# A new order for everything after the twentieth step of a fused attention and gated feed-forward kernel

## The chip, the cores and the metric

The kernel runs on one core of a Trainium2 chip. The metric is the device time of one execution in microseconds (us), as the median of several runs of the program. The core has five engines that each take their instructions in order from a queue of their own: PE (TensorE, matrix products; PEld is its loading of weights), DVE (VectorE), ACT (ScalarE), POOL (GpSimd) and SP (SyncE, which here only issues transfers). An engine whose next instruction waits for a semaphore does nothing else meanwhile, and all that stands behind that instruction waits too.

## The reference: what is computed

Two parts, one feeding the other. First a windowed attention with summaries of blocks of keys and values:

```python
k_sum = k.reshape(B, H, nb, block, D).max(axis=3)        # B, H, S, D = 4, 8, 768, 64; block 32
v_sum = v.reshape(B, H, nb, block, D).mean(axis=3)
scores_l = scale * np.matmul(q, k.transpose(0, 1, 3, 2)) # kept where |row - column| < 16
scores_s = scale * np.einsum('bhsd,bhnd->bhsn', q, k_sum) + np.log(block)
a = softmax(np.concatenate([masked scores_l, scores_s], axis=-1))
attn = np.matmul(a, np.concatenate([v, v_sum], axis=2))
```

Its output, 3072 tokens of 512 numbers, then goes through a feed-forward part with a gate that needs a cosine:

```python
h = x @ w_in            # (3072, 512) @ (512, 2048)
g = h * np.cos(h)
out = g @ w_out         # (3072, 2048) @ (2048, 512)
```

All of it is float32. (The code above is cut to what is computed.)

## The kernel before, in words

**Tiles.** The 3072 tokens are eight blocks of 384. For each block the attention is done by four groups (`Group`), one per pair of heads, named a, b, c, d with the block's number: c4 is the third pair of heads of block 4. The feed-forward part is done by 128 steps (`Step`), s0 to s127: a step is one block and one of the 16 slices of 128 columns of `w_in`. Blocks 0 and 1 share s0 to s31, then blocks 2 to 7 have 16 steps each: s48 to s63 are block 3, s80 to s95 block 5, s112 to s127 block 7. Products are taken with operands split into a high and a low part (`fp32r`), three products for one.

**What a step does.** `up` (L738) makes 12 products of 128x384 on PE into one bank of PSUM; this is `h`. Then follows a chain over two engines: `tu` (L748, ACT), `re` (L751, DVE), `si` (L756, ACT, the sine), `ga` (L760, DVE, the product with `h`), `hi` (the high part `gh`: L383 on ACT, or L385 on DVE) and `lo` (the low part `gl`: L389 on POOL or DVE). `dh` (L789) makes six products of 128x512 from `gh`, and `dl` three from `gl`, into three accumulating banks. At a block's last step `ta` (L825 on ACT, L827 on DVE) copies the three accumulators with a minus sign to SBUF, and `st` (L841) writes them out. The very last chunk is written in two halves (L845), one from SP's queue and one from ACT's. The tiles `t`, `gh` and `gl` have two buffers each, so that `hi` of a step can wait for `dh` of an earlier one.

**What a group does** (from block 2 on): `q` and `k` load, `qt` and `kt` (DVE) transpose, `kw` copies windows of the keys, `sc` (L581, PE) makes the scores, `z` (L601, DVE) scales and masks, `mx` (L614, DVE), `su` (L617, POOL), `ex` (L631, ACT), `sm` (L635, DVE), `iv` (L638, DVE) and `nm` (L641, POOL) are the softmax, `pt` (L664, DVE) transposes in squares of 32, `po` (L672) writes the result to DRAM, and `pi` (L679, four transfers) reads it back in another arrangement. `v` (L489 twice and L497 once) and `m` (L510, two transfers) load the values and their summaries into the tile `vn`. `va` (L694, PE) makes the attention's output, from which `xh` (L383 or L385) and `xl` (L389, DVE) are the two parts of `x` that the next block's `up` reads. The tiles `vn` and `pt` of these blocks have one buffer each: `v`, `m` and `pi` of one group cannot be issued before `va` of the group ahead has ended.

**What sets the order.** Nothing is scheduled automatically. A long string, `ORDER`, holds 2079 tokens such as `s22.dh.1.6.7` (step 22, first products of the down projection, in banks 1, 6 and 7) or `s23.lo.v` (low part of step 23 on VectorE), and a loop calls the method of each token in turn. Each engine gets its instructions in this order; the last part of a token names the banks of PSUM or the engine (`a` ACT, `v` DVE, `p` POOL).

```python
        for token in ORDER.split():
            who, what, *args = token.split(".")
            one = whose[who]
```

Of the kernel before, what the change touches and what calls it, by code (L numbers as in the profile page):

```python
# [67 lines left out]
s21.dh s21.dl s23.tu s23.re s21.ta.1.1.v s22.up.0 c2.ks.0 c2.kw.v c2.sc.7.2 a2.va.3 s21.st.1 d2.q b2.v s22.tu s23.si  # L68
s22.re s22.si s21.ta.2.0.v b2.sm s22.ga s21.st.2 s22.hi.a c2.z.0.v s23.ga b2.iv c2.z.1.v d2.ks.0 s22.lo.p b2.nm
d2.kw.a b2.pt.1 s26.up.4 s24.up.0 s24.tu c2.mx s24.re s23.hi.a s23.lo.v s27.up.2 s25.up.5 s26.tu s21.ta.0.0.v s24.si  # L70
s24.ga c2.su c2.ex s22.dh.1.6.7 s24.hi.v s22.dl s23.dh s23.dl s24.dh b2.m v2_2.l b2.po c2.sm s26.re s26.si s24.lo.p
v2_2.s.p b2.pi d2.qt a3.q v2_3.l s25.tu s25.re s25.si s24.dl c2.iv s26.ga s25.ga s25.hi.a d2.sc.0.4 b2.va.5 c2.v c2.m
a2.xh.a b2.xh.a d2.z.0.v d2.z.1.v c2.nm s25.lo.p s26.hi.v s27.tu c2.pt.1 s27.re s27.si s27.ga a3.kw.v b2.xl d2.mx
c2.po a3.qt v2_3.s.p v2_4.l c2.pi s21.st.0 s28.up.0 s31.up.4 s30.up.2 s29.up.5 d2.su d2.ex d2.sm d2.iv s26.lo.p
v2_4.s.v s28.tu s28.re d2.nm d2.pt.1 s25.dh s25.dl s27.hi.a s26.dh s26.dl s27.dh s27.lo.p s27.dl s28.si s28.ga s29.tu
s29.re s29.si s28.hi.v s29.ga s29.hi.v a2.xl s28.lo.p s31.tu a3.sc.0.5 c2.va.3 d2.po s31.fe.1.0 b3.q v2_5.l d2.m d2.pi
# [24 lines left out]
s54.tu s51.dh s51.dl s52.dh s52.dl d4.qt s53.ga s54.re s54.si d4.kw.a s53.hi.v s53.lo.v s53.dh c4.z.1.v s54.ga
s54.hi.a s54.lo.p s53.dl s54.dh c4.mx c4.su c4.ex c4.sm c4.iv d4.sc.0.1 d4.z.1.v a5.q b4.po v3_2.l a4.va.2 b4.m b4.v
s55.up.4 s55.tu c4.nm c4.pt.0 s55.re v3_2.s.v s55.si s55.ga s55.hi.a s59.up.1 s56.up.5 b4.pi v3_3.l s55.lo.p s57.up.4
a5.qt d4.z.0.v s56.tu s56.re s56.si s56.ga s56.hi.v s54.dl s56.lo.p a4.xh.a s55.dh s55.dl s56.dh s56.dl s59.tu s59.re
a5.kw.a a4.xl s57.tu s59.si s57.re s57.si b4.va.0 b4.xh.a d4.mx s57.ga s59.ga s59.hi.v a5.sc.2.4 b4.xl a5.z.1.v b5.q
b5.qt v3_3.s.p c4.v c4.m v3_4.l c4.po s58.up.1 c5.q d4.su d4.ex s59.lo.p d4.sm b5.kw.v d4.iv a5.z.0.v d4.nm s57.hi.a
s57.lo.v s58.tu s58.re a5.mx d4.pt.1 d4.po s58.si s62.up.0 s60.up.2 s60.tu s63.up.4 s61.up.5 s57.dh s58.ga s58.hi.v
s57.dl s58.dh s58.lo.v s58.dl s59.dh s59.dl s60.re s60.si s60.ga s60.hi.a s60.lo.v s62.tu s62.re s61.tu s61.re s61.si
s61.ga s61.hi.v s61.lo.v s62.si s62.ga s60.dh s62.hi.v s63.tu s63.re s63.si v3_4.s.p v3_5.l v3_5.s.p c4.pi c4.va.2
d4.v d4.m d4.pi b5.sc.5.1 b5.z.0.v c5.qt c4.xh.v v3_6.l s60.dl s62.lo.p s61.dh s61.dl s62.dh s62.dl s63.ga c4.xl a5.su  # L110
c5.kw.a a5.ex s63.hi.v s63.dh a5.sm s63.lo.p s63.dl c5.sc.0.2 a5.iv a5.nm a5.pt.0 a5.po d4.va.4 d4.xh.v d4.xl c5.z.0.v
# [5 lines left out]
s67.dl s68.dh s68.lo.p s70.tu s68.dl s70.re d5.sc.6.1 d5.z.1.v s70.si s70.ga c5.sm s70.hi.v a5.va.2 s70.lo.v a5.xh.a
a5.xl s69.up.1 s69.tu s69.re s69.si s73.up.0 s72.up.2 b5.m b5.v c5.iv d5.z.0.v s69.ga s69.hi.a s69.lo.p a6.ks.0
a6.ks.1 a6.kw.a s73.tu s69.dh s69.dl s70.dh s70.dl a6.qt s71.tu s71.re s71.si c5.nm c5.pt.1 d5.mx s71.ga s71.hi.a
s71.lo.v s72.tu s72.re s72.si s72.ga s72.hi.v b5.pi b5.va.6 b5.xh.v s72.lo.v d5.su d5.ex s73.re s73.si b6.kt.0 d5.sm  # L120
b6.kt.1 s73.ga a6.sc.3.1 a6.z.0.v s71.dh s71.dl s72.dh s72.dl s78.up.2 s76.up.0 s77.up.3 s76.tu s73.hi.a b5.xl
a6.z.1.v s76.re a6.mx b6.ks.1 s73.lo.p s76.si s76.ga s74.up.6 s74.tu d5.iv d5.nm s74.re s74.si s74.ga s74.hi.v
s74.lo.p s75.up.0 s75.tu s75.re s79.up.1 c5.po c5.m b6.q c5.v c6.k c5.pi c5.va.6 s73.dh s73.dl s74.dh s75.si s75.ga
s75.hi.a d5.pt.1 d5.po d5.m d5.v d5.pi s75.lo.p b6.ks.0 s77.tu s77.re s76.hi.a s74.dl s76.lo.v s77.si s78.tu c6.kt.0
s78.re s78.si s75.dh s75.dl s76.dh b6.qt s77.ga s77.hi.v s78.ga c6.kt.1 s78.hi.v s76.dl s77.lo.v s79.tu s79.re
# [869 lines left out]
```

## Time and profile before

| | |
|---|---|
| time before | 638.99 us, median of 3 runs: 634.86, 638.99, 639.19 |
| the profiled execution | span of 633.6 us from its first to its last instruction; 12128 instructions |
| PE | busy 620.6 us (98%) |
| DVE, ACT, POOL | busy 426.8 us (67%), 315.7 us (50%), 208.7 us (33%) |
| chain that ended last | 91% of the span on PE |
| PE's clock as granted | at least nine tenths of full speed in each of 40 slices; 1.00 on average over the stretches below |

The page gives the span of the profiled execution; its time with what lies around the span is not listed apart. The lowest of the three timed runs is 1.3 us above that span, the median 5.4 us. Matrix products overlap in the profile: one of 128x384 is listed with 337 ns, but the next starts about 175 ns later. So the time that PE needs for a piece of work is read from the chain of waits, where 12 of them take about 2.1 us, and not from the mean of one.

### The profile page before, as it was taken

The page shows a single profiled execution, that of the slowest core. Times are in us where ns is not written, and L with a number is a line of the kernel's source. Part 1 is how long each engine was busy: PE and PEld are TensorE (multiplying, and loading weights), DVE is VectorE, ACT ScalarE, POOL GpSimd, SP SyncE. Part 2 cuts the span into 40 slices and gives each one's busy share as a digit, 9 for nine tenths or more (in the row PEclk, how much of TensorE's full clock was granted, in tenths as well). Part 3 has the DMA queues.
Part 4 walks back from the last instruction along what each step waited for, and adds up shares of the span by engine and source line. Part 5 has one row for each costly group of instructions (what it writes and reads, how often), then busy time and mean ns, then how long its engine had stood idle before and what let it go on. Part 6 is the DMA issues. An engine that isn't in the chain of part 4 may idle for free.

```text
span 633.6 us, 12128 instructions
## 1 busy us (share of the span) xinstructions
PE 620.6 (98%) x4596; PEld 546.6 (86%) x4596; DVE 426.8 (67%) x795; ACT 315.7 (50%) x557; POOL 208.7 (33%) x243
## 2 busy tenths in 40 slices
PE   7889999999999999999999999999999999999997
PEld 5469898988889989897998989898888998989895
DVE  5689889986767877766766576657775555554524
ACT  3588776765544454464534554353554352522323
POOL 3136543563532523243434432211432241201000
PEclk9999999999999999999999999999999999999999
DMA  8987876734354465434343544232242313300001
GB/s 218 289 235 203 283 238 187 164 80 109 104 157 123 100 152 117 110 87 115 77 128 98 134 109 109 72 78 62 72 116 87 100 47 98 93 25 34 17 1 50
DMA packets 171305, 74.10 MB, mean 117 GB/s; under 512 B 136944, under 2 KB 160112, under 8 KB 171248
## 3 DMA queue, kind: packets, MB, share of 16 engines
q1 hardware_dynamic: 171104, 73.21, 43.6%
q8 instruction: 36, 0.59, 0.4%
q14 instruction: 21, 0.17, 0.1%
q10 hardware_dynamic: 144, 0.13, 0.1%
HBM read 54.43 MB, written 16.52 MB: 112 GB/s over the span
## 4 chain that ended last, share of the span: by engine, by line
PE 91%; SPq 3%; DVE 2%; DMA 2%; ACT 1%; POOL 0%; issue 0%; DVEq 0%; ACTq 0%
PE banks L738 41%; PE banks L789 41%; PE banks L694 4%; PE banks L581 3%; DMA late<-in_moe_w_out_dram 2%; SPq L468 2%; PE banks L650 1%; PE banks L593 0%; ACT L756 0%; SPq L497 0%; SPq L906 0%; SPq L489 0%; ACT t L756 0%; DVE t L760 0%; DVE xl L389 0%
## 5 line engine op out<-in xcount | busy, mean ns | idle before, releaser
L738 PE MATMUL banks<-xh,w 128*128 128x384 f32 x1024 | 267.0, 337 | 0.0
L789 PE MATMUL banks<-w,gh 128*128 128x512 f32 x768 | 197.4, 392 | 0.6 <-DVE stage L827 0.6
L738 PEld LDWEIGHTS banks<-xh,w 128*128 128x128 f32 x1024 | 185.3, 188 | 2.4 <-issue 1.3
L738 PE MATMUL banks<-xl,w 128*128 128x384 f32 x512 | 171.1, 334 | 0.0
L789 PEld LDWEIGHTS banks<-w,gh 128*128 128x128 f32 x768 | 142.7, 188 | 31.4 <-issue 1.2
L389 POOL TENSOR_TENSOR gl<-t,gh 128x384 fp32r<-128x384 f32 x67 | 68.7, 1029 | 240.2 <-DVE gh L385 84.6
L748 ACT ACTIVATE t<-banks 128x384 int32<-128x384 f32 x128 | 62.3, 489 | 162.4 <-PE banks L738 88.0
L751 DVE SCALAR_TENSOR_TENSOR t<-t,banks 128x384 f32<-128x384 int32 x128 | 69.7, 547 | 66.7 <-ACT t L748 66.3
L789 PE MATMUL banks<-w,gl 128*128 128x512 f32 x384 | 108.7, 391 | 0.0
L760 DVE TENSOR_TENSOR t<-t,banks 128x384 f32<-128x384 f32 x128 | 69.6, 548 | 41.9 <-ACT t L756 40.2
L756 ACT ACTIVATE t<-t 128x384 f32<-128x384 f32 x128 | 66.3, 523 | 63.0 <-DVE t L751 62.7
L738 PEld LDWEIGHTS banks<-xl,w 128*128 128x128 f32 x512 | 96.1, 188 | 0.3
L789 PEld LDWEIGHTS banks<-w,gl 128*128 128x128 f32 x384 | 71.8, 188 | 15.3 <-issue 0.2
L641 POOL TENSOR_TENSOR sc<-sc,r 128x720 f32<-128x720 f32 x28 | 40.1, 1432 | 58.6 <-DVE r L638 54.5
L383 ACT CAST gh<-t 128x384 fp32r<-128x384 f32 x62 | 31.4, 510 | 35.3 <-DVE t L760 19.2
L617 POOL TENSOR_TENSOR sc<-sc,m 128x720 f32<-128x720 f32 x24 | 34.0, 1415 | 44.5 <-DVE m L614 41.3
L389 DVE TENSOR_TENSOR gl<-t,gh 128x384 fp32r<-128x384 f32 x61 | 38.9, 640 | 11.5 <-ACT gh L383 6.6
L385 DVE CAST gh<-t 128x384 fp32r<-128x384 f32 x66 | 25.3, 383 | 15.8 <-PE banks L789 12.5
L254 POOL TENSOR_TENSOR kn<-kn 96x256 f32<-96x256 f32 (+1 forms) x38 | 25.7, 677 | 23.7 <-DMA kn<-in_v_dram 22.0
L601 DVE SCALAR_TENSOR_TENSOR sc<-banks,mask 128x360 f32<-128x360 f32 x48 | 24.2, 519 | 13.4 <-PE banks L581 13.4
L635 DVE TENSOR_REDUCE r<-sc 128x6 f32<-128x726 f32 x28 | 25.1, 897 | 10.0 <-ACT sc L631 9.6
L664 DVE STREAM_TRANSPOSE stage<-sc 128x768 f32<-128x768 f32 x24 | 23.3, 970 | 10.5 <-POOL sc L641 10.2
(115 smaller groups left out, 558.0 us busy)
## 6 DMA issues: line engine op xcount, KB each, us to landing
pd<-stage SPq DMA_DIRECT2D x24, 384.0 KB
late<-in_moe_w_out_dram SPq DMA_DIRECT2D x16, 511.6 KB
late<-in_moe_w_in_dram SPq DMA_DIRECT2D x16, 510.5 KB
pt<-pd SPq DMA_DIRECT2D x72, 96.0 KB
vn<-in_v_dram SPq DMA_DIRECT2D x50, 120.0 KB
out_dram<-stage SPq DMA_DIRECT2D x23, 256.0 KB
kn<-in_v_dram SPq DMA_DIRECT2D x24, 192.0 KB
qn<-in_q_dram SPq DMA_DIRECT2D x96, 48.0 KB
```

Source lines behind the costliest of these rows:

```text
L254: eng.tensor_tensor(out=t[:, :n], in0=t[:, :n], in1=t[:, n:], op=ALU.add)
L383: eng.copy(out=out, in_=in_)
L389: eng.tensor_tensor(out=lo, in0=src, in1=hi.bitcast(F32), op=ALU.subtract)
L617: nc.gpsimd.tensor_tensor(out=self.sc, in0=self.sc, in1=self.m.unsqueeze(2).broadcast_to([P, U, NK]), op=ALU.subtract)
L641: nc.gpsimd.tensor_tensor(out=self.sc, in0=self.sc, in1=self.r.unsqueeze(2).broadcast_to([P, U, NK]), op=ALU.mult)
L694: nc.tensor.matmul(out=self.xps[rows, t * QT : (t + 1) * QT], lhsT=self.vn[:, t, rows], rhs=self.pt[2 * c + hh][s], start=True, stop=True,)
L738: nc.tensor.matmul(out=self.h, lhsT=w_of(name, self.f)[:, c * P : (c + 1) * P], rhs=x_of(self.blk, part, c), start=n == 0, stop=n == last,)
L748: nc.scalar.activation(out=self.t.bitcast(I32), in_=self.h, func=AF.Copy, scale=1.0 / TWO_PI, bias=0.25)
L751: nc.vector.scalar_tensor_tensor(out=self.t, in0=self.t.bitcast(I32), scalar=-TWO_PI, in1=self.h, op0=ALU.mult, op1=ALU.add)
L756: nc.scalar.activation(out=self.t, in_=self.t, func=AF.Sin, scale=-1.0, bias=-0.5 * math.pi)
L760: nc.vector.tensor_tensor(out=self.t, in0=self.t, in1=self.h, op=ALU.mult)
L789: nc.tensor.matmul(out=self.acc[i], lhsT=g[:, i * P : (i + 1) * P], rhs=w_of(name, self.f), start=self.first and n == 0, stop=self.last an ...
```

## The change

From the token after `a2.va.3` on, all tokens stand in a new order up to the end; the 560 tokens ahead of that, which load and split the weights and do the steps up to s20 and most of s21, are as they were. The tokens are the same 2079 operations. With the new order some banks are others, and some of the operations that can run on two engines change sides: of the low parts (`lo`) 14 go from DVE to POOL and 13 from POOL to DVE, of the high parts (`hi`) 12 from ACT to DVE and 10 back, and five of the copies of key windows (`kw`) and four of the high parts of `x` (`xh`) change too. No function is changed, and no operation is added or removed. The first lines of the table that differ:

```diff
-s21.dh s21.dl s23.tu s23.re s21.ta.1.1.v s22.up.0 c2.ks.0 c2.kw.v c2.sc.7.2 a2.va.3 s21.st.1 d2.q b2.v s22.tu s23.si
+s21.dh s21.dl s23.tu s23.re s21.ta.1.1.v s22.up.0 c2.ks.0 c2.kw.v c2.sc.7.2 a2.va.3 s23.si s23.ga s23.hi.a s23.lo.v
```

Three places in the built programs are spoken of below. The first is DVE between the copies of key windows for c2 (`kw`) and the copy of the first accumulator of step 21 (L827, `stage_2002` before and `stage_1999` after). `gl` is the low part of step 23. Before, it is the last instruction ahead of that copy:

```order
L601 SCALAR_TENSOR_TENSOR sc<-banks,mask 128x3x120
L551 TENSOR_REDUCE kd_119<-kd_119 128x12
L664 STREAM_TRANSPOSE stage_1941<-sc 128x6x4x32
L614 TENSOR_REDUCE m<-sc 128x6
L751 SCALAR_TENSOR_TENSOR t<-t,banks 128x384
L389 TENSOR_TENSOR gl<-t,gh 128x384
L827 TENSOR_SCALAR stage_2002<-banks 128x512
```

In the changed program it follows the copies of the windows at once, behind the gate (L760) of the same step:

```order
L385 COPY kw<-kd_118 128x6x96
L385 COPY kw<-kd_118 128x6x24
L760 TENSOR_TENSOR t<-t,banks 128x384
L389 TENSOR_TENSOR gl<-t,gh 128x384
L751 SCALAR_TENSOR_TENSOR t<-t,banks 128x384
L635 TENSOR_REDUCE r<-sc 128x6
L760 TENSOR_TENSOR t<-t,banks 128x384
L827 TENSOR_SCALAR stage_1928<-banks 128x512
```

The same instructions stand between the window copies and the copy of that accumulator in both programs; the low part moved from their end to their start.

The second place is PE between the attention products of c4 and of d4 (L694, `va`), in block 4. L581 are scores of other groups; the products with `w_1347`, `w_1566`, `w_1718` and `w_1595` belong to steps 60, 61, 62 and 63. Before:

```order
L694 MATMUL banks<-pt,vn 64x64 x12
L581 MATMUL banks<-kw,qd 64x120 x12
L789 MATMUL banks<-w_1347,gl 128x512 x3
L789 MATMUL banks<-w_1566,gh 128x512 x6
L789 MATMUL banks<-w_1566,gl 128x512 x3
L789 MATMUL banks<-w_1718,gh 128x512 x6
L789 MATMUL banks<-w_1718,gl 128x512 x3
L789 MATMUL banks<-w_1595,gh 128x512 x6
L789 MATMUL banks<-w_1595,gl 128x512 x3
L581 MATMUL banks<-kw,qd 64x120 x12
L694 MATMUL banks<-pt,vn 64x64 x12
```

Now:

```order
L789 MATMUL banks<-w_1347,gl 128x512 x3
L581 MATMUL banks<-kw,qd 64x120 x12
L694 MATMUL banks<-pt,vn 64x64 x12
L789 MATMUL banks<-w_1566,gh 128x512 x6
L789 MATMUL banks<-w_1566,gl 128x512 x3
L789 MATMUL banks<-w_1718,gh 128x512 x6
L789 MATMUL banks<-w_1718,gl 128x512 x3
L789 MATMUL banks<-w_1595,gh 128x512 x6
L789 MATMUL banks<-w_1595,gl 128x512 x3
L581 MATMUL banks<-kw,qd 64x120 x12
L694 MATMUL banks<-pt,vn 64x64 x12
```

The scores of b5 and the low products of step 60 went ahead of c4's attention products, so that less of PE's work lies between those of c4 and those of d4. A row of 12 such products in this list is 24 in the trace.

The third place is the end of SP's queue, where the output is written. `stage_6593` and `stage_6596` before are chunks 0 and 1 of the last block, `last` the first half of chunk 2:

```order
L841 DMA out_dram<-stage_6221 128x512
L841 DMA out_dram<-stage_6083 128x512
L841 DMA out_dram<-stage_6346 128x512
L841 DMA out_dram<-stage_6593 128x512
L841 DMA out_dram<-stage_6596 128x512
L845 DMA out_dram<-last 128x256
```

Now `stage_6593` is chunk 1 and `stage_6600` chunk 0:

```order
L841 DMA out_dram<-stage_6133 128x512
L841 DMA out_dram<-stage_6083 128x512
L841 DMA out_dram<-stage_6513 128x512
L841 DMA out_dram<-stage_6593 128x512
L845 DMA out_dram<-last 128x256
L841 DMA out_dram<-stage_6600 128x512
```

The write of chunk 0 went from the third last place to the last, behind the half of the last chunk. The other half, on ACT's queue, is where it was.

More of the change, by code (lines that the diff above doesn't have):

```diff
@@ L72 @@
[L72 to L76, printed above, removed]
@@ L102 @@
[L102 to L106, printed above, removed]
@@ L107 @@
[L107 to L111, printed above, removed]
@@ L117 @@
[L117 to L121, printed above, removed]
@@ L122 @@
[L122 to L125, printed above, removed]
-s78.lo.v s77.dh s79.si s79.ga s79.hi.v b6.kw.a c5.xh.a s77.dl s78.dh s78.dl s79.dh a6.su s79.lo.p s79.dl c5.xl a6.ex
@@ L167 @@
-s126.re s124.hi.a s124.lo.v s125.tu s124.dh s124.dl s126.si s125.re s125.si s125.ga s125.hi.v s125.dh s126.ga
-s125.lo.v s126.hi.a s126.lo.v s127.tu s127.re s127.si s127.ga s125.dl s126.dh s126.dl s127.hi.v s127.dh s127.lo.v
-s127.dl s127.ta.0.0.v s127.st.0 s127.ta.1.1.a s127.st.1 s127.ta.2.a s127.st.2 s127.sb.2
+s21.dh s21.dl s23.tu s23.re s21.ta.1.1.v s22.up.0 c2.ks.0 c2.kw.v c2.sc.7.2 a2.va.3 s23.si s23.ga s23.hi.a s23.lo.v
+d2.q s22.tu s22.re s21.st.1 b2.sm s22.si s22.ga s21.ta.2.0.v s21.st.2 s22.hi.a s22.lo.p d2.ks.0 c2.z.0.v b2.iv b2.nm
@@ new lines @@
+c2.z.1.v d2.kw.a b2.pt.1 s26.up.4 s24.up.0 s24.tu s25.up.5 c2.mx s24.re s27.up.2 s26.tu s21.ta.0.0.v s24.si s24.ga
+c2.su c2.ex s22.dh.1.7.6 b2.v s24.hi.v s22.dl s23.dh s23.dl s24.dh v2_2.l b2.m b2.po s26.re s26.si s24.lo.p s24.dl
+d2.qt b2.pi v2_2.s.p v2_3.l s25.tu c2.sm a3.q c2.iv s26.ga s25.re s25.si d2.sc.0.4 s25.ga s25.hi.a b2.va.5 c2.v c2.nm
+c2.m b2.xh.a a2.xh.a s25.lo.p d2.z.0.v c2.pt.1 d2.z.1.v s26.hi.v s27.tu s27.re s27.si s27.ga a3.kw.v b2.xl d2.mx
+s28.up.0 v2_3.s.p a3.qt v2_4.l v2_4.s.v s21.st.0 s31.up.4 s30.up.2 d2.su c2.po d2.ex s29.up.5 d2.sm d2.iv c2.pi
@@ new lines @@
+s108.si s108.ga s108.hi.a s108.dh s108.lo.p s108.dl s110.tu s109.hi.v s109.dh s109.lo.p s109.dl s111.tu d7.v s110.re
+s110.si s110.ga s110.hi.a s110.lo.p c7.xh.v s110.dh c7.xl s111.re s111.si s111.ga s111.hi.v s110.dl s111.dh d7.m
+s111.lo.p s111.dl s111.ta.2.1.v d7.po d7.pi d7.va.3 d7.xh.v d7.xl s113.up.5 s113.tu s113.re s112.up.3 s111.ta.0.0.v
+s116.up.1 s114.up.4 s118.up.0 s112.tu s112.re s112.si s112.ga s112.hi.v s112.lo.p s116.tu s113.si s113.ga s113.hi.v
+s113.lo.p s116.re s116.si s116.ga s112.dh.6.2.3 s112.dl s113.dh s113.dl s116.hi.v s116.lo.v s114.tu s118.tu s115.up.5
@@ new lines @@
+s114.re s114.si s114.ga s114.hi.v s114.lo.v s118.re s115.tu s118.si s114.dh s114.dl s115.re s115.si s115.ga s115.hi.v
+s115.lo.p s117.up.1 s117.tu s117.re s115.dh s115.dl s116.dh s116.dl s117.si s117.ga s117.hi.v s117.lo.v s118.ga
+s118.hi.v s118.lo.p s120.up.5 s122.up.4 s123.up.0 s123.tu s119.up.1 s123.re s123.si s120.tu s117.dh s117.dl s111.st.0
+s120.re s123.ga s123.hi.v s123.lo.v s118.dh s118.dl s121.up.0 s119.tu s119.re s119.si s119.ga s119.hi.v s119.dh
+s119.lo.v s119.dl s120.si s120.ga s122.tu s126.up.1 s122.re s122.si s120.hi.a s120.lo.p s120.dh s121.tu s121.re
```

158 lines of the change are left out of this document (85 added, 73 removed).

## The prediction

> **What bounds the kernel now.** I read the page first, then a table of busy time by stretches, then PE's own waits.
>
> ```profile
> span 633.6 us, 12128 instructions
> PE 620.6 (98%) x4596; PEld 546.6 (86%) x4596; DVE 426.8 (67%) x795; ACT 315.7 (50%) x557; POOL 208.7 (33%) x243
> PE 91%; SPq 3%; DVE 2%; DMA 2%; ACT 1%; POOL 0%; issue 0%; DVEq 0%; ACTq 0%
> ```
>
> PE is busy almost throughout and is 91% of the chain that ended last. Where it is not busy matters most, so I cut the span into four stretches: the loading of weights, the rest of the unchanged part, the part that gets the new order, and what follows the last product. After the stretch's length come the busy times of PE, PEld, DVE, ACT and POOL, the granted clock, the share of the transfer engines and GB/s.
>
> ```profile
> 0.00:48.00 48.00, 40.07 (x645) 28.46 (x646) 34.37 (x73) 29.12 (x73) 13.33 (x42) 1.00 0.92 249
> 48.00:144.70 96.70, 96.70 (x616) 87.01 (x615) 86.08 (x139) 68.85 (x115) 52.16 (x50) 1.00 0.67 189
> 144.70:629.30 484.60, 483.80 (x3338) 431.17 (x3336) 306.30 (x585) 217.21 (x371) 143.22 (x151) 1.00 0.35 89
> 629.30:633.60 4.30, 0.00 (x0) 0.00 (x0) 0.00 (x0) 0.53 (x1) 0.00 (x0) 0.96 0.51 183
> ```
>
> In the third stretch, the only one with a new order, PE is busy 483.80 of 484.60 us at full clock. No product is added, removed or resized, so an order can win there only the 0.80 us of idle time, and perhaps a tenth or two in hidden short waits. It can lose as much as it likes. The 7.93 us of idle time before 48 us are out of its reach, and the 4.3 us behind the last product are touched only by the order of three writes. Of the 0.80 us, one wait makes 0.6 (us in total, times, longest):
>
> ```profile
> PE banks L789 <- DVE stage L827: 0.6, 1, 0.6
> ```
>
> **The change part by part.** First that wait. PE, DVE and POOL around it:
>
> ```profile
> 161.11 0.34 PE L738 MATMUL banks<-xh,w 128*128 128x384 f32 x1
> 162.06 1.62 PE L789 MATMUL banks<-w,gh 128*128 128x512 f32 x6 [0.62 <-DVE stage L827]
> 151.84 0.55 DVE L751 SCALAR_TENSOR_TENSOR t<-t,banks 128x384 f32<-128x384 int32 x1 [1.20 <-ACT t L748]
> 159.81 1.50 DVE L389 TENSOR_TENSOR gl<-t,gh 128x384 fp32r<-128x384 f32 x1
> 161.24 0.68 DVE L827 TENSOR_SCALAR stage<-banks 128x512 f32<-128x512 f32 x1
> 159.51 1.39 POOL L617 TENSOR_TENSOR sc<-sc,m 128x720 f32<-128x720 f32 x1 [1.88 <-DVE m L614]
> L389 DVE TENSOR_TENSOR gl<-t,gh 128x384 fp32r<-128x384 f32 x61 | 38.9, 640 | 11.5 <-ACT gh L383 6.6
> L383 ACT CAST gh<-t 128x384 fp32r<-128x384 f32 x62 | 31.4, 510 | 35.3 <-DVE t L760 19.2
> ```
>
> PE's products end at 161.45 and `dh` of s22 waits until the copy of the first accumulator of s21 has ended (161.92). Just ahead of that copy on DVE the low part of s23 took 1.50 us, where 61 of its kind have a mean of 640 ns; POOL ran a subtraction of 1.39 us from 159.51 on. In the new order the low part stands behind the copies of the key windows, 0.64 us long if POOL lets it, and the rest of the set before the accumulator's copy is the same. That alone frees 1.50 - 0.64 = 0.86 us, more than the 0.62 of the wait. Against that, DVE now stands still for the cast on ACT (510 ns) between gate and low part, but before it stood still at the same place for 1.20 us waiting for ACT. I take -0.6 us; the other end is +0.5, if that cast comes on top and the saving fails. Behind the moved low part are queued a residue and a sum on DVE; PE needs neither before the accumulator's copy.
>
> [...]
>
> Second, the loads of the values. `vn` and `pt` have one buffer, so for d4 nine transfers start after the products of c4. SP and PE before:
>
> ```profile
> 335.38 0.85 SPq L489 DMA_DIRECT2D vn<-in_v_dram  x2
> 336.29 0.48 SPq L497 DMA_DIRECT2D vn<-in_v_dram  x1
> 336.82 1.66 SPq L510 DMA_DIRECT2D vn<-vs  x2
> 338.60 1.84 SPq L679 DMA_DIRECT2D pt<-pd  x4
> 334.44 0.92 PE L694 MATMUL banks<-pt,vn 120*64 120x64 f32 x24
> 336.87 1.53 PE L789 MATMUL banks<-w,gh 128*128 128x512 f32 x6
> 343.86 0.92 PE L694 MATMUL banks<-pt,vn 120*64 120x64 f32 x24
> SPq L679 <- DMA pd<-stage: 12.1, 9, 2.1
> ```
>
> The products of c4 end at 335.36, the last issue at 338.60 + 1.84 = 340.44: 5.08 us of issuing. The landing has no row of its own. It is at most 343.86 - 340.44 = 3.42 us, since PE did not wait for it, and the nearest row is SP's wait for `pd`, at most 2.1 us. So 7.2 us are needed (5.1 to 8.5). In the new order the scores of b5 and three products of s60 no longer lie between, and what is left is the stretch from 336.87 to 343.86, 7.0 us. That is a wait of 0.2 us where 1.3 us were spare. The same happens once more, from b6 to c6: between them now stand scores, two steps of `dh` and `dl` and one `up`.
>
> ```profile
> 343.16 0.78 PE banks L581 x24
> 461.22 6.84 PE banks L789 x30
> 473.25 1.84 SPq L679 DMA_DIRECT2D pt<-pd  x4
> 469.68 8.52 PE banks L738 x48
> 468.98 1.73 SPq L510 DMA_DIRECT2D vn<-vs  x2
> ```
>
> 0.78 + 18 x 0.228 + 12 x 0.178 = 7.0 us. Before, the nine issues for c6 ran from 468.98 to 475.09, 6.1 us, while PE had until 469.68 + 8.52 = 478.2: at most 3.1 us for landing. With 5.1 + 2.1 = 7.2 the wait is 0.2, with 6.1 + 3.1 it would be 2.2. All other pairs of this kind have more of PE's work between them. From a6 to b6 there are 10.6 us (four `up` of 8.52 / 4 = 2.13, one step of 9 x 0.228 = 2.05), but two loads of b6's summaries now stand ahead of its `po` in SP's queue, and wait for a6. Two of them (1.66), `po` (0.4, as one write below), its landing (2.1), four and three more (1.84 + 1.33) and a landing (2.1) make 9.4: 1.2 to spare. I take +0.4 for all; the ends are 0 and 1.5 + 2.2 = 3.7.
>
> Third, the end. The write of chunk 0 is now behind the first half of chunk 2.
>
> ```profile
> 628.33 0.69 DVE L827 TENSOR_SCALAR stage<-banks 128x512 f32<-128x512 f32 x1 [1.44 <-PE banks L789]
> 629.05 0.81 SPq L841 DMA_DIRECT2D out_dram<-stage  x2
> 629.95 0.40 SPq L845 DMA_DIRECT2D out_dram<-last  x1
> 630.00:631.00 1.00, 0.00 (x0) 0.00 (x0) 0.00 (x0) 0.00 (x0) 0.00 (x0) 1.00 1.02 373
> 631.00:632.00 1.00, 0.00 (x0) 0.00 (x0) 0.00 (x0) 0.00 (x0) 0.00 (x0) 1.00 1.03 368
> ```
>
> Chunk 0 was ready at 629.02 and its issue began at 629.05; now it begins at 630.35. From issue to flowing data it is about 0.95 us (629.05 to 630.0), so its 256 KB flow from 631.3, and at some 370 GB/s they take 0.7 us: until 632.0, when the data ended before. But the engines idle a little at 630, as only chunk 1 is there. I take +0.2; ends 0 and 0.7, one whole chunk late.
>
> Fourth, shorter leads. From the end of `up` to `dh` of the same step the new order has eight steps with only two other steps' work (4.1 us) on PE between them: s56, s69, s80, s86, s95, s100, s110, s115. Before there are two, s69 and s118. How s69 went (ACT, DVE, PE):
>
> ```profile
> 373.78 0.49 ACT L748 ACTIVATE t<-banks 128x384 int32<-128x384 f32 x1 [1.81 <-DVE xl L389]
> 375.44 0.56 DVE L760 TENSOR_TENSOR t<-t,banks 128x384 f32<-128x384 f32 x1
> 376.03 0.52 ACT L383 CAST gh<-t 128x384 fp32r<-128x384 f32 x1 [0.62 <-DVE t L760]
> 377.69 1.08 PE L789 MATMUL banks<-w,gh 128*128 128x512 f32 x4
> L756 ACT ACT_TABLE_LOAD x23 | 29.5, 1283 | 0.4
> L631 ACT ACTIVATE sc<-sc 128x720 f32<-128x720 f32 x24 | 19.4, 807 | 10.7 <-POOL sc L617 10.5
> ```
>
> The chain from `tu` to `gh` took 2.77 us, and 1.14 us were left before `dh`. In the order none of the eight has an exponential between its own `tu` and `si`, and between `re` and `ga` stand at most two operations of attention on DVE, as for s69. I take 0; that cover is gone when more than 1.1 us comes between.
>
> The sum: -0.6 + 0.4 + 0.2 + 0 = 0 us, a span of 633.6 as before. The median of the runs is 5.4 us above the profiled span (638.99 - 633.6), the lowest run 1.3; I carry the 5.4 over, for no row tells what it is made of. Forecast: 639.0 us.
>
> **The rivals.** (a) Those 5.4 us are waits in the reordered part that the profiled execution was spared. A new order could be free of them, down to 639.0 - 5.4 + 1.3 = 634.9, or 0.8 less with every idle moment gone. For it speaks the spread of the three runs; against it, that the part before 48 us, with the transfer engines at a share of 0.92, is the likelier place, and unchanged.
>
> (b) Slower: the short leads break. If an exponential with its two table loads (1.283 + 0.807 + 1.283 = 3.37 us) gets ahead of `si`, `dh` is 3.37 - 1.14 = 2.2 us late. Three of the eight decide it, 639.0 + 6.6 = 645.6, just over 1%; half of them give 647.8. ACT's busy share of 50% and the order, as read above, speak against it.
>
> (c) The values come late at both places by the upper ends: 639.0 + 3.7 - 0.4 = 642.3. For it speak the 6.1 us of issuing at c6, against it that a transfer share of 0.35 in that stretch leaves room.
>
> **How the numbers follow.** The forecast has 0.68, (a) 0.11, (b) 0.10, (c) 0.11. The range goes from 634.0, the low end of (a), to 644.0, which holds (c) with the tail's 0.5 and the first term's 1.1 on top; (b) and a little more are left out. A change of 1% (6.4 us) is about what a measurement of this kernel can tell from none. The forecast, (a) and nearly all of (c) stay within it: 0.84. Slower by more has (b) and a rest of (c): 0.12. Faster by more would need more than the idle time there is: 0.04.
>
> **What would show it.** Right: in the changed profile PE has under 1.5 us of idle time between 144.7 us and its last product, the wait for L827 at s22 is gone, `va` of d4 and c6 show a wait for a transfer of a few tenths or none, and the last issue on SP is a write of `stage`. Wrong: PE rows with gaps of a microsecond or more ahead of L789 put down to ACT or DVE (b), or ahead of L694 put down to transfers (c), or the median at 635 with the same span (a).

## The result and the profile after

The changed kernel takes 641.88 us (median of 17 runs, 638.61 to 647.39), the kernel before, beside it on the same chips, 635.47 us (median of 17 runs, 633.25 to 640.89). The ratio is 1.0082 with a 95% interval of 1.0057 to 1.0107: slower by about 5 us (the two medians are 6.4 apart), which is under 1%, but clear of no change. The profiled execution of the changed kernel has a span of 638.9 us and a time of 640.62; in all 17 runs the time is the span plus 1.7 to 1.8 us.

First the page's lines on engines and on the chain of waits, then the two rows of the table by stretches in which the order differs (length, busy time of PE, PEld, DVE, ACT and POOL, granted clock, transfer share, GB/s):

```profile
span 638.9 us, 12147 instructions
PE 623.9 (98%) x4596; PEld 547.8 (86%) x4596; DVE 423.5 (66%) x794; ACT 315.9 (49%) x557; POOL 210.4 (33%) x244
PE 87%; SPq 4%; DMA 4%; DVE 3%; ACT 1%; issue 1%; POOL 0%; DVEq 0%; ACTq 0%; POOLq 0%
...
144.70:634.60 489.90, 485.68 (x3337) 431.43 (x3335) 302.95 (x584) 217.04 (x371) 145.42 (x152) 1.00 0.34 88
634.60:638.90 4.30, 0.00 (x0) 0.00 (x0) 0.00 (x0) 0.43 (x1) 0.00 (x0) 0.96 0.50 183
```

The stretch with the new order is 489.90 us long in place of 484.60, so it holds the whole difference of the spans. Of its 5.3 us, 3.4 are idle time of PE (489.90 - 485.68 = 4.22, before 0.80) and 1.9 are time in which PE counts as busy (485.68 in place of 483.80) for nearly the same work. The last row begins at a rounded time. Counted from the end of the last product, what follows took 4.36 us before and 4.51 now.

PE's own waits in that stretch (total, times, longest):

```profile
PE banks L694 <- DMA vn<-in_v_dram: 1.5, 1, 1.5
PE banks L694 <- DVE t L751: 1.3, 1, 1.3
PE banks L738 <- DVE t L760: 0.6, 1, 0.6
PE banks L789 <- DVE gh L385: 0.4, 1, 0.4
PE banks L789 <- DVE stage L827: 0.2, 1, 0.2
```

Five waits of 4.0 us in all, and the 0.6 us wait of before at `dh` of s22 is no longer among them. Each of the five leads back to SP's queue, as the experiments below show. First SP and PE around `va` of d2:

```profile
185.18 1.73 SPq L510 DMA_DIRECT2D vn<-vs  x2
187.01 0.47 SPq L672 DMA_DIRECT2D pd<-stage  x1
189.47 2.58 SPq L679 DMA_DIRECT2D pt<-pd  x4
192.10 0.88 SPq L489 DMA_DIRECT2D vn<-in_v_dram  x2
193.02 0.49 SPq L497 DMA_DIRECT2D vn<-in_v_dram  x1
195.78 0.92 PE L694 MATMUL banks<-pt,vn 120*64 120x64 f32 x24 [1.46 <-DMA vn<-in_v_dram]
```

In the new order the write `po` of d2 (L672) stands behind the loads `m` (L510), which cannot be issued before `va` of c2 has ended at 185.16. So the write goes out at 187.0, its read-back `pi` (L679) waits 2.0 us for it to land, and the values (L489, L497) stand behind `pi`. Before, `po` came ahead of `m`, and 5.7 us before it, as these two lines of the kernel before show:

```profile
180.88 0.34 SPq L672 DMA_DIRECT2D pd<-stage  x1
186.56 1.73 SPq L510 DMA_DIRECT2D vn<-vs  x2
```

Second, `va` of c6:

```profile
472.19 2.70 SPq L679 DMA_DIRECT2D pt<-pd  x4
474.99 1.67 SPq L510 DMA_DIRECT2D vn<-vs  x2
476.70 1.05 SPq L489 DMA_DIRECT2D vn<-in_v_dram  x2
477.80 0.49 SPq L497 DMA_DIRECT2D vn<-in_v_dram  x1
478.78 0.55 DVE L751 SCALAR_TENSOR_TENSOR t<-t,banks 128x384 f32<-128x384 int32 x1 [1.03 <-ACT t L748]
480.32 0.92 PE L694 MATMUL banks<-pt,vn 120*64 120x64 f32 x24 [1.33 <-DVE t L751]
```

The wait is put down to DVE, but the operation named had ended at 479.33, a microsecond before PE went on. The last values were issued until 478.29 and landed 1.9 us later (the last of their completion events is at 480.23); PE started 0.1 us after that.

Third, the place around s55 and s56, on DVE, ACT and PE:

```profile
306.67 1.07 DVE L264 TENSOR_REDUCE part_sum<-kn 96x64 f32<-96x512 f32 x1 [2.22 <-DMA kn<-in_v_dram]
307.99 0.54 DVE L751 SCALAR_TENSOR_TENSOR t<-t,banks 128x384 f32<-128x384 int32 x1
308.56 0.53 ACT L756 ACTIVATE t<-t 128x384 f32<-128x384 f32 x1 [2.52 <-DVE t L751]
309.73 0.44 PE L738 MATMUL banks<-xh,w 128*128 128x384 f32 x1 [0.63 <-DVE t L760]
314.63 1.64 PE L789 MATMUL banks<-w,gh 128*128 128x512 f32 x6 [0.44 <-DVE gh L385]
```

DVE stood still for 2.22 us at the sum of a tile of values for the block summaries, whose load `v3_2.l` had moved on SP from ahead of `pi` of b4 to behind it. First its issue before, then its issue now:

```profile
295.90 0.37 SPq L249 DMA_DIRECT2D kn<-in_v_dram  x1
303.62 0.33 SPq L249 DMA_DIRECT2D kn<-in_v_dram  x1
```

The residue of s55 (L751), the sine on ACT and the gate (L760) were late by as much; an `up` waited 0.63 us for its bank, and `dh` of s56 0.44 us for its `gh`. The fifth wait, at `dh` of s48 (0.16 us here), is for the copy of the third accumulator of s47; the experiments show what is behind it.

### The profile page after: what moved, and what is told of

Same layout as the page of the kernel before. It is cut to its first block, busy times and chain, and to the rows that moved or that the text cites. A ratio compares the mean times of both kernels' runs of the same rounds, so it can differ in the third digit from the quotient of the medians.

```text
span 638.9 us, 12147 instructions
## 1 busy us (share of the span) xinstructions
PE 623.9 (98%) x4596; PEld 547.8 (86%) x4596; DVE 423.5 (66%) x794; ACT 315.9 (49%) x557; POOL 210.4 (33%) x244
## 4 chain that ended last, share of the span: by engine, by line
PE 87%; SPq 4%; DMA 4%; DVE 3%; ACT 1%; issue 1%; POOL 0%; DVEq 0%; ACTq 0%; POOLq 0%
PE banks L789 40%; PE banks L738 39%; PE banks L694 4%; PE banks L581 3%; SPq L468 2%; DMA late<-in_v_dram 1%; DMA late<-in_moe_w_out_dram 1%; PE banks L650 1%; SPq L679 1%; DMA out_dram<-stage 0%; PE banks L593 0%; DMA kn<-in_v_dram 0%; PE banks L914 0%; DMA vn<-in_v_dram 0%; DVE t L751 0%
## 5 line engine op out<-in xcount | busy, mean ns | idle before, releaser
L738 PE MATMUL banks<-xh,w 128*128 128x384 f32 x1024 | 271.0, 337 | 0.6 <-DVE t L760 0.6
L389 POOL TENSOR_TENSOR gl<-t,gh 128x384 fp32r<-128x384 f32 x68 | 70.1, 1033 | 231.3 <-DVE gh L385 116.2
L751 DVE SCALAR_TENSOR_TENSOR t<-t,banks 128x384 f32<-128x384 int32 x128 | 69.3, 547 | 66.0 <-ACT t L748 65.6
L760 DVE TENSOR_TENSOR t<-t,banks 128x384 f32<-128x384 f32 x128 | 69.6, 547 | 45.2 <-ACT t L756 43.9
L389 DVE TENSOR_TENSOR gl<-t,gh 128x384 fp32r<-128x384 f32 x60 | 34.1, 571 | 13.5 <-ACT gh L383 6.7
L385 DVE CAST gh<-t 128x384 fp32r<-128x384 f32 x68 | 27.1, 399 | 14.4 <-PE banks L789 10.2
```

The source lines that it names most:

```text
L385: eng.tensor_copy(out=out, in_=in_)
L389: eng.tensor_tensor(out=lo, in0=src, in1=hi.bitcast(F32), op=ALU.subtract)
L738: nc.tensor.matmul(out=self.h, lhsT=w_of(name, self.f)[:, c * P : (c + 1) * P], rhs=x_of(self.blk, part, c), start=n == 0, stop=n == last,)
L751: nc.vector.scalar_tensor_tensor(out=self.t, in0=self.t.bitcast(I32), scalar=-TWO_PI, in1=self.h, op0=ALU.mult, op1=ALU.add)
L760: nc.vector.tensor_tensor(out=self.t, in0=self.t, in1=self.h, op=ALU.mult)
```

## The experiments

The part up to step 21 is the same in all kernels, but step 21 ends between 147.5 and 151.0 us in the twelve traces. So the kernels are compared by a **stretch**: from the end of the last product of step 21 to the end of the last product of step 127 on PE, from each kernel's profiled execution; it is cut once at the end of step 79, around which both orders have the same 200 tokens. Where PE waits for nothing, this measure repeats: behind step 79 the four kernels with the order of before there (before, half, b_d2 and b_ta) take 213.35 to 213.37 us. Before it is 629.20 - 149.17 = 480.0 us, after 634.40 - 148.79 = 485.6. Ratios are those of the timed runs to the kernel before. By them none of the three single edits of the changed kernel can be told from it, so what one edit does is read from its trace.

| kernel | stretch | to step 79 | behind it | ratio, 95% interval |
|---|---|---|---|---|
| before | 480.0 | 266.7 | 213.4 | |
| after | 485.6 | 269.6 | 216.0 | 1.0082 (1.0057 to 1.0107) |
| u_d2 | 484.6 | 269.1 | 215.5 | 1.0066 (1.0041 to 1.0091) |
| u_v3 | 483.7 | 267.8 | 215.9 | 1.0067 (1.0039 to 1.0094) |
| u_c6 | 485.1 | 270.0 | 215.1 | 1.0096 (1.0061 to 1.0131) |
| u_all | 481.8 | 266.7 | 215.1 | 1.0023 (0.9998 to 1.0049) |
| u_fix | 480.3 | 265.8 | 214.6 | 1.0010 (0.9988 to 1.0032) |
| half | 479.1 | 265.7 | 213.4 | 0.9980 (0.9958 to 1.0002) |
| b_d2 | 483.6 | 270.3 | 213.4 | 1.0062 (1.0027 to 1.0097) |
| b_ta | 479.5 | 266.2 | 213.4 | 0.9992 (0.9974 to 1.0009) |
| alt | 513.2 | 280.8 | 232.5 | 1.0519 (1.0484 to 1.0555) |
| alt2 | 493.6 | 273.6 | 220.0 | 1.0207 (1.0181 to 1.0234) |

**One transfer put back: d2.** The theory: PE waits because transfers come late, each by its place in SP's queue. The rival: the waits are slack that moves on to something else.

```diff
-c2.va.3 d2.m d2.po d2.pi d2.v
+c2.va.3 d2.po d2.m d2.pi d2.v
```

> The changed kernel with one token put back: the write po of d2 goes ahead of m of d2 on SP again, as before the change. Theory (three late transfers, each with its own place): the wait of PE at va of d2 (1.46 us at 195.8 us in the changed kernel) goes, since po's write has landed by the time the loads m are issued, and pi follows them at once. Nothing else moves, so PE's idle time between 144.7 us and its last product falls from 4.2 to about 2.8 us and the span from 638.9 to 637.4. Rival (the wait only moves on: something behind it is late next): the wait at d2 goes but another of a microsecond or more appears on PE within the next 50 us, and the span stays at 638.4 to 638.9.

The wait at d2 went: by the end of step 47 the 1.5 us were won. But then 1.1 us were lost again at `dh` of s48, in the way of the rival, though 87 us later and not within 50. DVE and PE of this kernel there:

```profile
281.86 0.69 DVE L827 TENSOR_SCALAR stage<-banks 128x512 f32<-128x512 f32 x1 [2.56 <-DMA out_dram<-stage]
282.61 1.19 PE L789 MATMUL banks<-w,gh 128*128 128x512 f32 x4 [1.31 <-DVE stage L827]
```

The copy of the third accumulator waits on DVE for a write to `out_dram` to land, which has to release the tile that it copies into. That write is `st.0` of s47, and in the new order it stands on SP behind the loads `d4.q`, `a4.m` and `v3_1.l`. The landing did not move with PE: PE came 1.5 us sooner and stood 1.1 us longer. The stretch is 1.0 us shorter, not 1.5.

**The load of a value tile put back.**

```diff
-c4.ex b4.po b4.pi c4.sm c4.iv v3_2.l s55.up.4
+c4.ex b4.po v3_2.l b4.pi c4.sm c4.iv s55.up.4
```

> The changed kernel with one token put back: the load v3_2.l of a key tile goes ahead of pi of b4 on SP, as before the change. Theory (late transfer): DVE no longer stands still for the 2.22 us ahead of the maximum of that tile at 306.7 us, so the gate of s55 is in time for the next up in its bank (0.63 us of PE's idle time) and gh of s56 for dh of s56 (0.44 us); with the slower products behind each wait that is 1.2 to 1.4 us, span 637.6. Rival (the leads of s55 and s56 are simply too short in the new order, 4.1 us with two other steps' work): the wait for the gate goes, but dh of s56 still waits 0.4 us or more for gh, and the span is 638.2 or longer.

(The text calls `v3_2.l` the load of a key tile and the operation a maximum; it loads values, and L264 is a sum.) DVE of this kernel at that sum:

```profile
303.35 1.04 DVE L264 TENSOR_REDUCE part_sum<-kn 96x64 f32<-96x512 f32 x1
```

The standstill went, and with it both waits of PE, that for `gh` of s56 too: the short lead was enough once nothing stood in DVE's way. The stretch is 1.9 us shorter, more than the 1.2 to 1.4 expected: 0.3 us of it are the 24 score products of a5, which take 1.16 us in the changed kernel and 0.85 in this one, with no wait listed in either. d2's wait was 0.2 us shorter in this execution, and the one at s48 0.3 us longer.

**The products of c6 two products later.**

```diff
-c6.v c6.va.6 d6.m s91.hi.a a7.su s94.tu s94.re s91.lo.p s93.tu s91.dh s91.dl
+c6.v s91.hi.a a7.su s94.tu s94.re s91.lo.p s93.tu s91.dh s91.dl c6.va.6 d6.m
```

> The changed kernel with va of c6 two products later: behind dh and dl of s91 (and the load m of d6, which waits for it, behind it). Theory (late transfer): the values of c6 land at about 480.2 us and the 2.05 us of dh and dl of s91 cover that, so the 1.33 us of PE's idle time at 480.3 go and the span is 637.5. d6 has 13.3 us between its va and that of c6, so its loads still come in time. Rival (the wait is for DVE, which the row names, and gh of s91 comes off the same row of operations on DVE): dh of s91 waits instead, by about a microsecond, and the span stays within 0.5 us of 638.9.

The 1.33 us went, and `dh` of s91 followed its `up` with no wait, so DVE was not what PE had waited for. In their place d6 now waited 0.39 us, for `pt<-pd`, because its loads start after c6. Behind step 79 the stretch is 0.9 us shorter; ahead of it, which the edit does not touch, it is 0.4 us longer, as the waits of the new order are not the same in every execution (that at s48 was 0.16 us in the changed kernel and is 0.36 here). The timed runs, with five of this kernel, cannot tell it from the changed kernel.

**All three.**

> The changed kernel with all three edits (po of d2 ahead of m, v3_2.l ahead of pi of b4, va of c6 behind dl of s91). Theory: the three add up, 1.5 + 1.3 + 1.4 = 4.2 us, a span of 634.7 and a ratio to the kernel before of about 1.0015; PE's idle time from 144.7 us to its last product is under 0.5 us. What is left above 633.6 is then no wait but longer products: PE's steps from one product to the next are a few nanoseconds longer behind each change between up and down products, and the new order changes between them some 50 times more often. Rival 1 (no such price): the span is 633.2 or less, since the 0.6 us at s22 that the new order won stay won. Rival 2 (the waits were slack that others shared): the span stays above 636.

The stretch is 3.8 us shorter than with the changed kernel, not 4.2, since the wait at s48 (0.4 us) and the new one at d6 (0.4 us) stand. What is left over before, 1.8 us, is more than these two waits, although the order still has its gain at s22. By the letter the span of 636.4 us falls to rival 2 (above 636); but beside the changed kernel it is 0.9 us longer ahead of the end of step 21 and 0.4 behind the last product, where none of the edits reaches.

**Four edits.** In addition to the first two, `va` of c6 comes behind `dh` of s91 alone, and the write `st.0` ahead of `d4.q` (the text below counts `m` of d6, which follows `va` of c6, as a fifth transfer):

```diff
-... d4.q s49.ga ... b4.iv s47.st.0 s47.ta.2.0.v s47.st.2 s48.dh.6.3.7
+... s47.st.0 d4.q s49.ga ... b4.iv s47.ta.2.0.v s47.st.2 s48.dh.6.3.7
```

> The changed kernel with the order of five transfers mended: po of d2 ahead of m; v3_2.l ahead of pi of b4; va of c6 behind dh of s91 (not behind dl, which made d6 wait 0.4 us); and the write of the first chunk of s47 (st.0) ahead of the load d4.q on SP, since the copy of the third chunk, on which dh of s48 waited 0.4 to 1.3 us in all runs of this order so far, waits on DVE for that write to land. Theory: no wait of more than 0.2 us is left on PE from 144.7 us on; the stretch from the end of step 21 to the end of step 127, 480.0 us before and 481.8 with the first three edits, comes to about 480.8. That is still some 0.8 us more than before although the wait at s22 is gone, because of the changes between up and down products (22 more of them at about 65 ns). Rival 1 (no price for changes): 479.3 or less. Rival 2 (the copy waits for something else): dh of s48 still waits 0.4 us or more.

```profile
144.70:625.00 480.30, 480.30 (x3319) 428.29 (x3318) 301.55 (x581) 215.78 (x368) 145.27 (x152) 1.00 0.35 90
```

PE is busy in every hundredth of those 480.30 us: all five waits are gone, the one at s48 among them, and 5.3 us of the stretch with them. That is 1.3 us more than the waits listed. The rest is booked as busy, most of it for this reason: products overlap, but the last one ahead of a wait runs to its end with nothing behind it (its run-out). The `up` of s93, just ahead of the wait at c6, holds PE for 2.27 us in the changed kernel and for 2.11 here. So of the 5.6 us that the change cost in the stretch, 5.3 hang on the places of a few transfers and of c6's products. But the mended order has no wait and has won the one at s22, and still is 0.3 us longer than before: 0.9 us shorter up to step 79, 1.2 us longer behind it. Something there costs time while PE is busy.

**What it is: changes between up and down products.** In the order before, mostly three to eight `up` steps follow each other, and then two to seven steps of `dh` and `dl`. In the new order single `up` steps stand between single steps of `dh` and `dl`, above all behind step 79. In the stretch before there are 23 separate groups of `up` products, after 45; behind step 79 there are 10 and 28. The chain of waits of the mended order (first fence) and of the kernel *half* told of below, which has the order of before there (second fence), near the end; the columns are start, duration, and what:

```profile
599.97 2.10 PE banks L738 x12
602.08 2.08 PE banks L789 x9
604.16 2.10 PE banks L738 x12
606.26 2.08 PE banks L789 x9
```

```profile
602.16 12.50 PE banks L738 x72
614.67 13.42 PE banks L789 x59
```

A group takes a fixed time beside that of its products: from 2.10 = a + 12 s and 12.50 = a + 72 s come s = 173 ns and a = 20 ns for `up`; from 2.08 and 13.42, s = 227 ns and a = 39 ns for the others (the view ends at 628 us, so 59 products of that last group are in its row). Each additional pair of groups costs some 60 ns. (From the starts of all groups between others of the same kinds the medians are 26 and 39 ns, 65 together.) It shows in no row of waits, since PE is never idle.

To isolate this price I moved 29 `up` steps of the kernel before behind a later `dl` (the text below says 28, but its sum takes 29), such as these in the last block:

```diff
-s121.up.5 ... s127.up.3 s126.up.5 s124.up.1 ... s125.up.7 s121.dh s121.dl s122.dh s122.dl s123.dh s123.dl
+s121.up.5 ... s124.up.1 ... s121.dh s121.dl s125.up.7 s122.dh s122.dl s126.up.5 s123.dh s123.dl s127.up.3
```

> The kernel before with 28 of its up steps (s52 to s127) moved behind a dl, so that PE changes more often between the two kinds of products: 52 separate groups of up products in the new stretch in place of 23 (the changed kernel has 45). Engines, banks and the order on ACT, DVE, POOL and SP are those of before, and each moved up still has three steps' work between it and its dh. Theory (each additional group costs about 65 ns, 39 for the down group that is cut off and 26 for the up group): 29 x 65 = 1.9 us more from the end of step 21 to the end of step 127, 481.9 in place of 480.0 us, with no wait that names another engine. Rival (the longer products of the changed kernel come from its other neighbours on DVE, ACT and POOL, not from the changes): within 0.5 us of 480.0, apart from waits.

This missed: 33 us, not 1.9, and by waits that I had excluded. They come to 21.5 us, and PE ran at half its clock for 17 us behind the longest of them, as the last section shows. The three largest rows:

```profile
PE banks L789 <- DVE t L760: 5.6, 2, 4.0
PE banks L789 <- DVE stage L827: 5.4, 3, 2.5
PE banks L738 <- DVE t L760: 3.7, 5, 1.2
```

I read this from the places of the waits, without a run of its own: an `up` moved back takes its 2.1 us away from between the first `up` of a row and that step's own `dh`, and from between a block's last product and the copy of its accumulators. Of the 21.5 us, 0.7 are at steps that were moved (s57 and s89). Those that they had stood behind lost their lead. A milder form with 15 of them:

> The kernel before with 15 of its up steps (s40 to s127, at most two out of one row of them, so that gates, accumulator copies and values keep their time) moved behind a dl: 38 separate groups of up products in place of 23. Theory (65 ns for each additional group): 15 x 65 = 1.0 us more from the end of step 21 to the end of step 127, 481.0 in place of 480.0 us, with no wait over 0.3 us on PE but the one at s22, and each cut-off group of up products or down products some 26 or 40 ns longer than its place in a long row. Rival (the changes cost nothing; the changed kernel's products are longer by other neighbours): 480.0, within 0.2.

It still had waits of some 10 us, and the stretch 13.6 us more. Neither run isolates the price by its time. In both, the groups that no wait touches have the same medians, 26 and 39 or 40 ns.

**Half of each.** The mended order up to the first chain operation of step 75, and the order of before from there on:

> The mended changed order up to the first chain operation of step 75, and from there on the order of the kernel before: it has the new order's gain at s22 and few changes between up and down products behind s75. Theory (the price of the changes lies in the part behind step 79, where the mended order has most of them and no wait): the stretch from the end of step 21 to the end of step 127 takes 479.1 us, 0.9 less than before and 1.2 less than with the mended order throughout; the ratio to the kernel before is about 0.9985. Rival (that 1.2 us came from something left behind by the first part, such as transfers or buffers): the stretch stays at 480.0 us or more.

```profile
144.70:629.00 484.30, 484.29 (x3342) 431.87 (x3340) 302.81 (x587) 218.96 (x373) 140.95 (x149) 1.00 0.35 89
```

The stretch is 479.05 us as expected (479.1), 1.27 us less than with the mended order throughout, 1.21 of it behind step 79. The two differ by 18 groups of `up`, and 18 x 0.065 = 1.17 us. The price fits in size and place. Product by product the two traces bear it out: counted from start to start, 1.20 of the 1.21 us lie between products of `up`, `dh` and `dl`, and 0.01 in all scores and values. Behind a change to `dh` the first three products take 2.6, 6.6 and 9.2 ns over 226.7 in *half*, and 2.5, 6.5 and 9.1 in the mended order, so a group costs the same in both and only their number differs. Why PE takes longer behind a change stays open. This kernel has the lowest median of all, 634.37 us (12 runs) against 636.04 for the kernel before beside it, a ratio of 0.9980; but its interval reaches 1.0002, so it is not shown to be faster.

**One part alone in the kernel before: d2.**

```diff
-c2.va.3 d2.po s31.fe.1.0 b3.q v2_5.l d2.m d2.pi d2.v
+c2.va.3 d2.m d2.po s31.fe.1.0 b3.q v2_5.l d2.pi d2.v
```

> The kernel before with one token moved: the loads m of d2 stand ahead of the write po of d2 on SP, as in the changed kernel. Theory (this alone makes the wait at d2): po now waits on SP for va of c2, and pi for po's write to land, so va of d2 waits 1.2 to 1.5 us for its values; the stretch from the end of step 21 to the end of step 127 goes from 480.0 to about 481.4 us. Rival (the wait also needs the changed order of PE's products around it): no wait of more than 0.3 us at va of d2.

The wait appears with this move alone, and is larger than expected (total, times, longest):

```profile
PE banks L694 <- DMA vn<-in_v_dram: 2.0, 1, 2.0
```

The stretch, however, is 3.6 us longer, not 1.4 and not 2.0: the section on the hardware below shows the rest.

**One part alone in the kernel before: the low part at s22.**

```diff
-s23.hi.a s23.lo.v s27.up.2 s25.up.5 s26.tu s21.ta.0.0.v s24.si
+s23.hi.a s27.up.2 s25.up.5 s26.tu s21.ta.0.0.v s23.lo.v s24.si
```

> The kernel before with one token moved: the low part of s23 (L389, 1.50 us beside POOL's subtraction) stands behind the copy of the first accumulator of s21 on DVE instead of ahead of it. Theory (that low part alone held the copy): the 0.62 us of PE's idle time ahead of dh of s22 go, and the stretch from the end of step 21 to the end of step 127 goes from 480.0 to about 479.3 us; a ratio of 0.999. Rival (the copy comes up against the same POOL operation instead, or waits for its accumulator): the wait stays at 0.3 us or more.

DVE, POOL and PE of this kernel:

```profile
158.92 0.68 DVE L827 TENSOR_SCALAR stage<-banks 128x512 f32<-128x512 f32 x1
159.52 0.90 DVE L389 TENSOR_TENSOR gl<-t,gh 128x384 fp32r<-128x384 f32 x1
158.62 1.39 POOL L617 TENSOR_TENSOR sc<-sc,m 128x720 f32<-128x720 f32 x1 [1.88 <-DVE m L614]
160.39 1.55 PE L789 MATMUL banks<-w,gh 128*128 128x512 f32 x6
```

`dh` of s22 follows with no wait, and the copy takes its usual 0.68 us beside POOL's subtraction. By the end of step 24, 0.84 us were won; by the end of step 27, 0.35 of them were given back, so the stretch is 0.5 us shorter. In time it cannot be told from the kernel before.

## Why the forecast came out right, and where it did not

**The sum was wrong, and so was what it stood on.** I forecast a span of 633.6 and a time 5.4 us above it, 639.0. The span came to 638.9 and the time is 1.7 to 1.8 us above the span in every run. Errors of 5.3 us too little in the span and 3.7 too much above it partly cancel, and that is why 641.88 lies within 634.0 to 644.0: luck. With 1.7 us above the span the forecast would have been 635.3, the time of the kernel before. By the signs that I had set, the mechanism was wrong too. PE stood idle for 4.2 us and not under 1.5, `va` of c6 waited 1.33 us and not a few tenths, and `va` of d2 shows a microsecond's gap put down to a transfer, the sign of rival (c). Nor does a measurement need 1% to tell a change from none: the interval here is 0.25% to either side. The 5.4 us had been the median of three runs against one span; over 17 runs the kernel before has a median of 635.47, and 633.6 + 1.7 = 635.3 for the profiled execution is close to it. A single span and a median of three are not one sample, and the smaller offset was in the list: the lowest run, 1.3 us above.

**First term (-0.6 us): right.** The wait at s22 went in the changed kernel, and in the kernel before by moving the low part alone (-0.84 us by step 24, of which 0.5 stayed). That the wait of 0.62 us gave back 0.84 is the same run-out of the last product as above: the idle time listed was not all that an order could win. The low part takes 0.56 us at its new place with POOL idle:

```profile
151.37 0.56 DVE L389 TENSOR_TENSOR gl<-t,gh 128x384 fp32r<-128x384 f32 x1 [0.63 <-ACT gh L383]
```

Beside the same subtraction of POOL it ended 0.41 us behind it in both places where the two meet: 161.31 against 160.90 before, 160.42 against 160.01 in b_ta. It had met the subtraction with 1.09 us left of it before, and with 0.49 in b_ta, and took 1.50 and 0.90 us, so in these two places it ended by POOL's end and not by its own start. What ties the one to the other no run shows; that POOL alone had made the low part long, and that it would take 0.64 us elsewhere, was an estimate from its row of 1.50 us and the mean of 61 of its kind. The copy of the accumulator, which in b_ta ran beside the same subtraction (158.92 to 159.60 against 158.62 to 160.01), took 0.68 us, as in the kernel before with POOL's subtraction over.

**Second term (+0.4, up to 3.7): the step that failed.** Right was that PE would wait for loads of values, and that c6 is one of the places; its 1.33 us lie between the 0.2 that I took and the 2.2 that I named as the other end. I should have taken more: the row with 6.1 us of issuing stood there, and the issuing took 6.1 again (472.19 to 478.29), begun 0.4 us after the products of b6 had ended, with a landing of 1.9 behind it. At d4 there was no wait:

```profile
342.67 1.66 SPq L510 DMA_DIRECT2D vn<-vs  x2
346.48 0.74 PE L694 MATMUL banks<-pt,vn 120*64 120x64 f32 x17
```

From the end of the last issue (344.33) to the start of `va` there were 2.1 us, and the values had landed 0.8 us ahead of it. For b6 the forecast of no wait held. Wrong was the sentence "All other pairs of this kind have more of PE's work between them". It counts PE's work between two `va`, as if the loads of a group always took the same time. For d2 the work between did not change; what changed was that `po` fell behind `m` on SP, so that a landing of 2 us came into the row of transfers. I had looked for exactly that at b6, and not at d2: 1.46 us. Nor had I gone through the transfers that other engines wait for: `v3_2.l` for DVE (1.9 us in the stretch), and the write `st.0` for the copy of an accumulator (0.2 to 1.3 us).

**Third term (+0.2): right.** From the end of the last product to the end of the span it is 4.51 us in place of 4.36, with the write of chunk 0 as the last. In the six traces with the end of before it is 4.34 to 4.36; in the six with the new one it is 4.50 or 4.51 three times, 4.92 twice and 5.53 once.

**Fourth term (0 for the short leads): right.** Of the eight steps only s56 waited, and not once `v3_2.l` was back in its place.

**What had no term:** 22 more groups of `up` between `dh` and `dl`, some 60 ns each, 1.3 us. I had said that no product is resized and took their time as given; the rows to price a change by, groups of different length in the chain, were in the trace of before.

**The rivals.** (a) has nothing for it: 1.7 to 2.1 us lie outside the span in every run since, and what is left is spread between the spans of runs. In the traces that spread is in the unchanged part up to step 21 (147.5 to 151.0); where the runs without a trace lose theirs is not on record. (b) is false: no exponential broke a lead. (c), values late at two places, is what happened by its mechanism, 1.46 + 1.33 = 2.8 us where it gave 3.7, at d2 and c6 rather than d4 and c6, and it is half of the loss. My 0.68 stood on the sum of four terms that each looked at one place; two more places and one price were not looked at.

## What to carry to other kernels

When an order by hand changes, go through the transfer queue token by token before anything else: for each transfer note what it must wait for, what now stands ahead of it, and who waits for its landing, on every engine. Here a transfer that waits for another one's landing added 2.0 us to all that stood behind it. When a wait on PE went, the listed time was not all that was won: 0.84 us for 0.62 at s22 by step 24, and 5.3 for 4.0 in the stretch with all five gone, most of it because the product ahead of a wait overlaps the next again (2.11 us for the `up` of s93 in place of 2.27). And where PE is busy throughout, read its time per product from groups of different length, as above: what a change of kind costs, here some 60 ns for a pair of groups, shows in no row of waits.

## What the runs showed of the hardware

**A wait of 2 us cost nearly twice its length.** Granted clock and busy time of PE in the kernel b_d2, in slices around its wait at `va` of d2 (which ended at 198.30):

```profile
196.00:198.00 2.00, 0.27 (x12) 0.04 (x4) 0.53 (x1) 0.00 (x0) 1.08 (x3) 1.00 0.81 172
198.00:200.00 2.00, 1.70 (x25) 1.59 (x26) 0.30 (x1) 0.00 (x0) 0.00 (x0) 0.64 0.91 207
200.00:202.00 2.00, 2.00 (x8) 2.00 (x8) 1.93 (x4) 0.00 (x0) 0.00 (x0) 0.51 0.64 111
202.00:204.00 2.00, 2.00 (x13) 2.00 (x13) 0.60 (x2) 0.49 (x1) 1.39 (x1) 1.00 0.01 2
```

Behind the wait of 2.0 us PE's granted clock fell to half, from about 198.6 (where a mean of 0.64 over that slice puts it) to 202, some 3.4 us; products of 128x384 came 320 ns apart in place of 173. In that time the products of d2's `va` took 0.4 us longer than in the kernel before and the next `up` 1.1 us; with the wait of 2.0 that is nearly all of the 3.6 us. Behind the changed kernel's wait of 1.46 us at the same place the clock stayed at 1.00:

```profile
194.00:196.00 2.00, 0.54 (x20) 0.31 (x12) 0.58 (x2) 0.00 (x0) 0.00 (x0) 1.00 0.71 179
196.00:198.00 2.00, 2.00 (x32) 1.93 (x29) 1.22 (x3) 0.00 (x0) 0.00 (x0) 1.00 1.13 170
```

In the kernel alt all four waits of 2.2 us or more (2.19, 2.55, 3.95 and 2.71) had the same aftermath, the last twice as long, as another wait of 1.68 us fell into it: the granted clock is 0.50 from 283 to 285 us and from 444 to 446, behind two of them, and 0.987 over the whole run of 665.1 us, which is some 17 us at half. No wait of up to 1.46 us in the stretches had it, in any trace. In b_d2 the record of the clock begins at 3.99 us, and the clock changed at 198.55 and 201.97: 194.56 us lie between the first two, 57 times 3.413, and 3.42 between the others. In the trace of the kernel before the record has full clock for 628.05 us, from 5.24 us until behind the last product, and in that of the changed kernel for 631.47, with all five of its waits within them; these are 184 and 185 times 3.413. So when in such a piece of 3.4 us a wait falls may count; that is an estimate from these four lengths and was not tried, nor was a wait between 1.46 and 2.0 us at full clock.
